# A new hand-written emission order between the last lags and the first feed-forward block, and the skip term of the last two chunks added in PSUM

## The chip, the cores and the metric

The kernel runs on one core of a Trainium2 chip. The metric is device time of one execution in microseconds; lower is better. The core's engines are TensorE (PE: matmuls into PSUM, with its weight loads listed apart as PEld), VectorE (DVE: elementwise work), ScalarE (ACT: activations, copies with a scale), GpSimd (POOL) and SyncE (SP), which here issues nearly all DMAs. Each engine works through its own queue in order, and engines wait for each other by semaphores.

## The reference, cut to what matters

Two layers are run one after the other, each a state-space convolution and a SwiGLU block, both with a layer norm in front and a residual. L = 2048 positions, D = 512 channels, F = 1376 hidden columns, N = 128 states. Both layers share their weights.

```python
def _A_ref(u, ...):                       # u: (1, L, D)
    K = einsum("dn,dnl,dn->dl", Cc, exp(dt * A * l), dt * Bc).real    # (D, L) taps
    y = causal convolution of u with K along L, by FFT of length 2L
    return y + u * Dskip

def _B_ref(x, w_gate, w_up, w_down):
    return (silu(x @ w_gate) * (x @ w_up)) @ w_down

x = x + _A_ref(_layernorm(x), ...)
x = x + _B_ref(_layernorm(x), ...)
x = x + _A_ref(_layernorm(x), ...)
x = x + _B_ref(_layernorm(x), ...)
```

The skip term `u * Dskip` is the same as `Dskip` added to tap 0 of K, and that is how the kernel does it.

## The kernel before, in words

**Tiling.** Positions go in four blocks of 512 for each layer; the eight blocks are worked in the order `SEQ`, (layer, block): (0,0), (0,1), (0,2), (1,0), (0,3), (1,1), (1,2), (1,3). The convolution is done block by block with odd-frequency transforms of length 1024 as matmuls: the spectra of the taps and of the normed inputs are multiplied on DVE and transformed back on PE. Each spectrum is cut by channel half `h` (256 channels) and by frequency residue `q`, worked in the order 0, 2, 1, 3. A feed-forward block goes in two halves of 256 positions (`TB`); for each half PE makes gate and up products in PSUM (`pgu`), two hidden tiles at a time (L934, L935, L937: three half-precision products for one of near-single precision), then the down products `py` (L950 to L952).

**Taps.** The taps come in eight chunks of 64 channels. For each chunk DVE and ACT make powers; PE multiplies them to the lags, `pk` (`lags`, L514); ACT copies them to `ks` (`spread_in`, L525). For the first six chunks `ks` goes through DRAM to its final place `kt`. For the last two, 6 and 7, `spread_pe` does it: 16 products of 256 columns with slices of the identity move partition groups into the PSUM tile `kp` (L541), and ACT copies `kp` to `kt` (L543). Then `skip` (L521) adds `Dskip` to tap 0, which lies in partition 0: on DVE for chunks 0 to 6, on POOL for chunk 7. PE transforms `kt` to spectra: `spectra` for two residues at once (L549, combined on DVE in L577), `first_parts` (L594, copied by ACT in L595) for the part that block 0 needs, `later_parts` (L603, L605, which run L549) for the parts of the later blocks. The second variable that `later_parts` yields at is the point between the halves: one call of `take` emits products of the real part, the next those of the imaginary part, the third the combination (four ACT copies L612, L613, one DVE add L614, a store by SP).

**The stretch that is reordered** begins after `pk` of chunk 7 is emitted (L1175) and ends with the last line of the hand-written order (L1256). In it stand, as generators that `take(it, n)` advances by n steps:

- `conv[h]`: the convolution of block 0 for half `h`. Each of the first four steps makes one residue's product on DVE (L816, L824, L825); every second step adds L771 and L772. The fourth makes two inputs of the inverse transform (L837, then L840, L841) and has PE transform each (`pi`, L788). The fifth makes the other two (L845, L848, L849) and adds the first result to `x` (L797); the sixth adds the second.
- `tail["sp"]`: the end of `spectra` of chunk 6 (the add L577, then two stores).
- `first_parts(c, q)`: `c` is 7. The call for chunk 7 with q = 0 or 2 covers chunk 7; that for chunk `c - 1` with q = 1 or 3 covers chunks 6 and 7. `conv[1]` needs all four, its residues in the order q = 0, 2, 1, 3.
- `odd` and `rest`: `later_parts` of chunk 6 (q = 1, 3: six steps) and of chunk 7 (all q: twelve steps).
- `split(hi, lo, load)`: steps of preparing the feed-forward weights as two half-precision parts: a load by SP, the high part on ACT (L677; the first on DVE, L675), the residue on DVE (L682). Eight column groups come first, then eleven row groups of `w_down` (L702, L705), which are emitted after the stretch.
- `scales` and `tops`: small DVE work for the weights' scales (L359, L364 to L376). `last`: the last normed input's spectrum of block 1 (PE L316, ACT L319).
- `norm`: the layer norm ahead of the first feed-forward half: DVE statistics, a power on POOL (L214), the last factor on DVE (L217); then ACT's scaling (L868), PE's transposes (L870) and ACT's copy to `nh` (L873); then DVE's residue `nlo` (L875).
- `block1`: the convolution of block 1; its first step makes one residue's product.
- `direct_size`, `sizes`: maxima for a scale.

**What sets the order.** In the stretch PE, DVE, ACT and POOL take their instructions in the order in which the code emits them (`manual_schedule`). SP and everything emitted later are placed by the framework's planner, which simulates a timeline and can put later work between instructions of the hand-written order. Of the PSUM tiles, `kp`, `pt` and `pgu` share two large buffers (`pbig`), and the pieces of `later_parts`, the inverses and `pf` share two tags of two small ones (`psml`), which alternate from call to call:

```python
small = [itertools.cycle(("sml", "py"))]
def psml(shape, name):
    return ps.tile(shape, F32, name=name, tag=next(small[0]), bufs=2)
```

Of the kernel before, what the change touches and what calls it, by code (L numbers as in the profile page):

```python
# [32 lines left out]
DC = 64  # L33
NCH = D // DC
# [43 lines left out]
def kernel(ctx, tc, x, a_re, a_im, b_re, b_im, c_re, c_im, log_dt, d_skip,  # L78
                           w_gate, w_up, w_down, c_ef, c_ei, c_ek, c_am, c_eh, c_eih, out):
    nc = tc.nc  # L80
    V, A, G, PE = nc.vector, nc.scalar, nc.gpsimd, nc.tensor
# [9 lines left out]
    def tl(shape, name, tag, dt=F32):  # L91
        return sb.tile(shape, dt, name=name, tag=tag, bufs=BUFS[tag])

    def pbig(shape, name):
        return ps.tile(shape, F32, name=name, tag="big", bufs=2)
# [45 lines left out]
    ident = sb.tile([P, P], F32, name="ident")  # L141
# [49 lines left out]

    tdk = tl([P, 2, D], "tdk", "t")
    dsk, th32 = tdk[0:1, 0], tdk[:, 1]
    nc.sync.dma_start(dsk, d_skip)
    dmax = sb.tile([1, 1], F32, name="dmax")

    def direct_size():

        da = tl([1, D], "da", "sg")
        A.activation(da, dsk, AF.Abs)  # L200
        V.tensor_reduce(dmax, da, axis=AX.X, op=OP.max)
# [45 lines left out]
    def parted(t):  # L247

        return t.rearrange("p a b d -> p b a d")
# [60 lines left out]
    def direct(b, h, q, n, space=psml):  # L310

        pf = space([P, 2, HD], "pf")
        for i in range(2):
            for c in range(4):
                e = ek[q // 2][:, q % 2, c - 1, i] if c else ef[:, q, i]
                PE.matmul(pf[:, i], lhsT=e, rhs=n[c], start=c == 0, stop=c == 3)  # L316
        yield
        u = tl([P, NQ, 2, DC], "u", "uu")
        A.activation(parted(u), whole(pf), AF.Copy)  # L319
        nc.sync.dma_start(udr[0][b, h, q], u)  # L320
# [3 lines left out]
    def second(h, q, space=psml):  # L324
        if h not in halves:
            halves[h] = n = []
            for cp in range(2):
                t = tl([P, 2, HD], "n1", "uu")
                nc.sync.dma_start(t, ndr[h, cp])
                n += [t[:, 0], t[:, 1]]  # L330
        return direct(1, h, q, halves[h], space)
# [175 lines left out]
    def lags(ts, g):  # L507
        re, im = ts[:2]
        pk = pbig([P, 16, 64], "pk")
        for i, e in enumerate((re, im)):  # L510
            for dd in range(16):
                for grp in range(4):
                    d = 16 * grp + dd
                    PE.matmul(pk[32 * grp:32 * grp + 32, dd, :], lhsT=g[:, i, :, d], rhs=e[:, 0:64, d], start=i == 0 and dd % 8 == 0, stop=i == 1 and dd % 8 == 7,  # L514
                              tile_position=(0, 32 * grp))
        return pk

    def skip(ch, kt, eng):

        k = kt[0:1, :, 0]  # L520
        eng.tensor_tensor(k, k, dsk[:, ch * DC:(ch + 1) * DC].rearrange("p (g d) -> p g d", g=4), OP.add)  # L521

    def spread_in(pk):
        ks = tl([P, 4, 16, 16], "ks", "nn")
        A.activation(ks, pk.rearrange("p d (c a) -> p a c d", a=4), AF.Copy)  # L525
        return ks

    def spread(ch, ks, kt, eng=nc.sync):

        k = kdr[ch % 2]  # L530
        with tc.high_priority(offset=BOOST):
          eng.dma_start(k.rearrange("g b a f -> (g b) a f"), ks.rearrange("p a c d -> p a (c d)"))
          for ga in range(4):
            eng.dma_start(kt[32 * ga:32 * ga + 32].rearrange("p g c d -> p g (c d)"), k[:, :, ga].rearrange("g b f -> b g f"))

    def spread_pe(ks, kt):

        kp = pbig([P, 4, 16, 16], "kp")
        for grp in range(4):
            for ga in range(4):  # L540
                PE.matmul(kp[32 * ga:32 * ga + 32, grp], lhsT=ident[:, 32 * grp:32 * grp + 32], rhs=ks[:, ga],  # L541
                          start=True, stop=True, tile_position=(0, 32 * ga))
        A.activation(kt, kp, AF.Copy)  # L543

    def products(pw, kt, k0, k1, q, order):
# [41 lines left out]
    def first_parts(c0, q):  # L587

        n = NCH - c0
        pw = pbig([P, 2, 8, 4, 16], "pw")[:, :, :n]  # L590
        for c in range(4):
            for i in range(2):
                e = ek[q // 2][:, q % 2, c - 1, i] if c else ef[:, q, i]
                PE.matmul(pw[:, i], lhsT=e, rhs=kt2[:, c0 + 2 - NCH:, :, c], start=c == 0, stop=c == 3)  # L594
        A.activation(parted(w0r[:, 1, q, c0 % NQ:]), pw.rearrange("p i k g d -> p i k (g d)"), AF.Copy)  # L595
# [23 lines left out]
    def sizes(ch, kt, junk):  # L619

        A.activation(junk, kt, AF.Abs, accum_out=wsum[:, ch:ch + 1])
# [20 lines left out]
    def take(it, n):  # L642
        for _ in range(n):
            next(it, None)
# [101 lines left out]
    def ssm(layer, b):  # L746

        if (layer, b) == SEQ[INV]:
            nc.sync.dma_start(eih, c_eih)
        for h in range(2):  # L750
            yield from ssm_half(layer, b, h)
# [227 lines left out]
    with tc.manual_schedule(engines={mybir.EngineType.Activation, mybir.EngineType.DVE, mybir.EngineType.PE, mybir.EngineType.Pool}):  # L979
# [56 lines left out]
        def at(t, f, n=1):  # L1036
            plan.append((t, len(plan), (lambda: take(f, n)) if hasattr(f, "__next__") else f))

        def later(make):

            yield from make()
# [35 lines left out]
        def use(c, t):  # L1077

            box, kt, n = {}, kt2[:, c % 2], starts[c + 1]

            def copy():
                box["ks"] = spread_in(box["pk"])
                if c < NCH - 2:
                    spread(c, box["ks"], kt)
            at(t, lambda: box.update(pk=lags(ts[c], gs[c])))
            at(t + 7.1, copy)
            if c == NCH - 2:
                at(t + 10.0, lambda: spread_pe(box["ks"], kt))
            at(t + 13.1, lambda: skip(c, kt, V))
            at(t + 25.0, lambda: sizes(c, kt, box["ks"]))  # L1090
            for q0, ats in list(enumerate(((t + 17.5, t + 25.2, n + 2.1, n + 7.5),
                                      (n + 6.9, n + 14.0, n + 17.3, n + 21.0))))[:2 if c < NCH - 2 else 1]:
                sp = later(lambda q0=q0: spectra(c, kt, q0))
                if c == NCH - 2:
                    tail["sp"] = sp
                    ats = ats[:2]
                for t0 in ats:
                    at(t0, sp)
# [26 lines left out]
        tail = {}  # L1125
        starts = [0.0, 31.0, 62.0] + [93.0 + 28.0 * k for k in range(NCH)]
        for i in range(NCH - 1):
            t = starts[i]
# [12 lines left out]
        t = starts[NCH - 1]  # L1141
# [8 lines left out]
        c, kts = NCH - 1, (kt2[:, 0], kt2[:, 1])  # L1150
# [5 lines left out]
        nhl2 = mix[:, 4 * D:].bitcast(F16).rearrange("p (s i k t) -> p s i k t", s=2, i=2, k=4)  # L1156
# [9 lines left out]
        def split(hi, lo, load=0):  # L1166
            for _ in range(load):
                loads.pop(0)()
            for _ in range(hi):
                his.pop(0)()  # L1170
            for _ in range(lo):
                los.pop(0)()
# [9 lines left out]
        conv = [ssm_half(0, 0, h) for h in range(2)]  # L1182
# [7 lines left out]
        ks = spread_in(pk)  # L1190
        odd = later_parts(c - 1, kts[0], (1, 3))
        rest = later_parts(c, kts[1])
# [2 lines left out]
        ivs = iv[0] + iv[1]  # L1195
        norm = first_norm(tl([P, 2, D], "nn1", "hf"))
        last = second(*sec[-1])
        take(conv[0], 1)
        take(tail["sp"], 2)
        spread_pe(ks, kts[1])  # L1200
        skip(c, kts[1], G)
        take(conv[0], 1)
        while tops:
            tops.pop(0)()
        scales()
        split(1, 0)
        first_parts(c, 0)
        take(conv[0], 1)
        split(1, 1)
        split(0, 0, 1)  # L1210
        first_parts(c, 2)
        split(1, 0)
        take(conv[0], 1)
        first_parts(c - 1, 1)
        split(1, 0)
        take(last, 2)
        take(conv[1], 1)
        first_parts(c - 1, 3)
        take(conv[1], 1)
        split(0, 1)  # L1220
        split(0, 0, 1)
        take(conv[0], 1)
        take(conv[1], 1)
        split(1, 1)
        split(0, 0, 1)
        take(conv[1], 1)
        split(0, 1)
        split(0, 0, 1)
        take(odd, 2)
        take(conv[1], 1)  # L1230
        direct_size()
        block1 = ssm(0, 1)
        take(norm, 1)
        take(rest, 2)
        take(odd, 1)
        take(odd, 2)
        take(norm, 1)
        take(block1, 1)
        take(rest, 1)
        split(1, 0)  # L1240
        take(odd, 1)
        take(norm, 1)
        split(0, 1)
        take(rest, 3)
        take(conv[0], 1)
        take(conv[1], 1)
        ready = nhl2[:, 0, 0], nhl2[:, 0, 1]
        split(1, 1)
        take(rest, 3)
        split(1, 1)  # L1250
        take(rest, 4)
        split(0, 0, 3)
        sizes(c, kts[1], ks)
        nn2 = tl([P, 2, D], "nn2", "nn")
        nt3 = sb.tile([P, D], F16, name="nt3")
        parts = itertools.cycle([nn2[:, 1].bitcast(F16)[:, i * D:(i + 1) * D] for i in range(2)] + [nt3])  # L1256
# [54 lines left out]
```

## Time and profile before

| what | us |
|---|---|
| median of three runs (1073.61 to 1075.19) | 1075.15 |
| the profiled execution, whole | 1072.84 |
| its span, first to last instruction | 1071.1 |
| PE busy in the span | 1016.9 |
| DVE busy | 964.0 |
| ACT busy | 546.3 |
| POOL busy | 107.5 |

The profile gives each engine's instructions with start, duration and the releaser of the idle time before them. Matmuls are pipelined, so a row's duration is longer than its share of PE's time; the distance between two starts is what counts. A single-precision matmul shows as two rows. The table of windows gives the busy time in a stretch and the clock that was granted to PE (1.00 is full).

### The profile page before, as it was taken

What the parts mean: (1) busy time and instruction counts of PE and PEld (TensorE: products, weight loads), DVE (VectorE), ACT (ScalarE), POOL (GpSimd) and SP (SyncE); (2) the same over time, 40 slices, a digit from 0 to 9 for tenths busy, and PEclk for the clock granted to TensorE, in tenths of its full rate; (3) what the DMA queues carried; (4) which work ended last, traced back from release to release, by engine and by line L of the source; (5) the groups of instructions that cost most, each with busy time, mean ns of one, the idle gap of its engine ahead of it and who ended that gap; (6) DMA issues with size and microseconds to landing.
All of it is one profiled execution on the core that took longest, in us unless ns stands there. A gap on an engine that the chain in (4) does not pass through costs nothing.

```text
span 1071.1 us, 22000 instructions
## 1 busy us (share of the span) xinstructions
PE 1016.9 (95%) x8918; PEld 801.9 (75%) x8918; DVE 964.0 (90%) x1397; ACT 546.3 (51%) x1093; POOL 107.5 (10%) x169
## 2 busy tenths in 40 slices
PE   1979999998788999999999999999999999999998
PEld 1868888887686787777869687786868677696775
DVE  7999999999999999999999999999999999972221
ACT  6989888853367264466652126534526522153210
POOL 1112322320001011011000000200100000000000
PEclk9989999998899999999999999999999999999999
DMA  6366777878755354423054454453533344312000
GB/s 216 105 187 167 176 164 186 191 194 268 250 176 166 105 149 114 148 94 80 20 124 144 142 191 132 103 148 104 149 110 94 100 137 128 119 32 58 2 26 20
DMA packets 120199, 139.73 MB, mean 130 GB/s; under 512 B 50705, under 2 KB 75793, under 8 KB 119330
## 3 DMA queue, kind: packets, MB, share of 16 engines
q1 hardware_dynamic: 108098, 112.83, 35.1%
q0 software_dynamic: 12000, 25.50, 10.1%
q8 instruction: 70, 1.15, 0.5%
q14 instruction: 31, 0.25, 0.1%
HBM read 91.36 MB, written 30.67 MB: 114 GB/s over the span
## 4 chain that ended last, share of the span: by engine, by line
PE 58%; DVE 29%; ACT 5%; issue 3%; DMA 3%; POOL 1%; SPq 0%; DVEq 0%; ACTq 0%
PE pgu L934 10%; PE pgu L935 10%; PE pgu L937 10%; PE py L952 6%; PE py L951 6%; PE py L950 6%; DVE g L489 4%; PE pi L788 3%; DVE g L504 2%; DVE spare L501 2%; PE pf L284 2%; DVE wall L416 2%; DVE t L816 2%; PE pw L549 1%; DVE yk L819 1%
## 5 line engine op out<-in xcount | busy, mean ns | idle before, releaser
L934 PE MATMUL pgu<-mix,wall 128*128 128x256 f16 x1280 | 299.7, 273 | 1.6 <-ACT mix L873 1.1
L935 PE MATMUL pgu<-mix,wall 128*128 128x256 f16 x1280 | 299.5, 273 | 0.0
L937 PE MATMUL pgu<-mix,wall 128*128 128x256 f16 x1280 | 195.8, 273 | 0.0
L935 PEld LDWEIGHTS <-wall 128*128 128x128 f16 x1280 | 125.5, 98 | 17.9 <-issue 2.4
L934 PEld LDWEIGHTS <-wall 128*128 128x128 f16 x1280 | 125.4, 98 | 15.1
L937 PEld LDWEIGHTS <-wall 128*128 128x128 f16 x1280 | 125.2, 98 | 15.0
L950 PE MATMUL py<-wall,hh 128*128 128x512 f16 (+1 forms) x352 | 133.4, 379 | 0.0
L951 PE MATMUL py<-wall,hh 128*128 128x512 f16 (+1 forms) x352 | 133.4, 379 | 0.0
L952 PE MATMUL py<-wall,hl 128*128 128x512 f16 (+1 forms) x352 | 132.4, 379 | 0.0
L819 DVE TENSOR_TENSOR yk<-yk,t 128x1024 f32<-128x1024 f32 x96 | 116.9, 1218 | 0.4
L816 DVE TENSOR_TENSOR t<-uu,w 128x1024 f32<-128x1024 f32 x96 | 116.9, 1218 | 0.3
L940 ACT ACTIVATE sg<-pgu,sc 128x512 f32<-128x512 f32 x80 | 54.6, 682 | 98.1 <-PE pgu L937 95.1
L942 ACT ACTIVATE hh<-sg 128x512 f16<-128x512 f32 x80 | 50.2, 627 | 102.0 <-DVE sg L941 102.0
L941 DVE SCALAR_TENSOR_TENSOR sg<-pgu,sc,sg 128x512 f32<-128x512 f32 x80 | 59.6, 745 | 40.4 <-ACT sg L940 40.4
L549 PE MATMUL pw<-kt,ek 128*128 128x256 f32 (+1 forms) x384 | 94.0, 383 | 0.0
L549 PEld LDWEIGHTS pw<-kt,ek 128*128 128x128 f32 x384 | 75.4, 200 | 8.6
L952 PEld LDWEIGHTS <-hl 128*128 128x128 f16 (+1 forms) x352 | 34.3, 98 | 38.5
L943 DVE TENSOR_TENSOR hl<-sg,hh 128x512 f16<-128x512 f32 x80 | 54.9, 686 | 8.9 <-ACT hh L942 8.8
L951 PEld LDWEIGHTS <-hh 128*128 128x128 f16 (+1 forms) x352 | 34.5, 98 | 37.8
L950 PEld LDWEIGHTS <-hh 128*128 128x128 f16 (+1 forms) x352 | 34.4, 98 | 37.5
L514 PE MATMUL pk<-wall,g 128*32 128x64 f32 x2048 | 58.7, 287 | 1.9 <-issue 1.8
L514 PEld LDWEIGHTS pk<-wall,g 128*32 128x32 f32 x2048 | 55.9, 134 | 5.1 <-issue 5.0
(273 smaller groups left out, 1845.2 us busy)
## 6 DMA issues: line engine op xcount, KB each, us to landing
uu<-udr SPq DMA_DIRECT2D x96, 256.0 KB, 3.0
w<-wdr SPq DMA_DIRECT2D x96, 256.0 KB, 2.8
g<-g POOLq DMA_DIRECT2D x12, 512.0 KB, 7.2
udr<-fu POOLq DMA_DIRECT2D x22, 256.0 KB, 3.2
udr<-u SPq DMA_DIRECT2D x16, 256.0 KB, 3.3
kdr<-ks SPq DMA_DIRECT2D x6, 512.0 KB, 3.4
kt<-kdr SPq DMA_DIRECT2D x24, 128.0 KB, 3.1
out_dram<-xg SPq DMA_DIRECT2D x12, 256.0 KB, 2.3
```

Of the source, the lines that this page charges most:

```text
L514: PE.matmul(pk[32 * grp:32 * grp + 32, dd, :], lhsT=g[:, i, :, d], rhs=e[:, 0:64, d], start=i == 0 and dd % 8 == 0, stop=i == 1 and dd % 8 ...
L549: PE.matmul(pw[:, i], lhsT=e, rhs=kt[:, :, c + 4 * k0:4 * k1:4, :].rearrange("p g k d -> p k g d"), start=c == 0, stop=c == 3)
L816: V.tensor_tensor(t, uu.unsqueeze(2).to_broadcast([P, NQ, 2, 2, DC]), w.unsqueeze(3).to_broadcast([P, NQ, 2, 2, DC]), OP.mult)
L819: V.tensor_tensor(yk, yk, t, OP.add)
L934: PE.matmul(o, lhsT=wgu(wi, k, 0)[:, fs], rhs=nh[:, k], start=k == 0, stop=False)
L935: PE.matmul(o, lhsT=wgu(wi, k, 1)[:, fs], rhs=nh[:, k], start=False, stop=False)
L937: PE.matmul(o, lhsT=wgu(wi, k, 0)[:, fs], rhs=nlo[:, k], start=False, stop=k == 3)
L941: V.scalar_tensor_tensor(sg, pgu[:, 1], sc6[:, 4:5], sg, OP.mult, OP.mult)
L943: V.tensor_tensor(hl[:, f0:f0 + 2], sg, hh[:, f0:f0 + 2], OP.subtract)
L950: PE.matmul(py[r], lhsT=hh[:n, f, rc], rhs=wd(f, 0)[:n], start=f == 0, stop=False)
L951: PE.matmul(py[r], lhsT=hh[:n, f, rc], rhs=wd(f, 1)[:n], start=False, stop=False)
L952: PE.matmul(py[r], lhsT=hl[:n, f, rc], rhs=wd(f, 0)[:n], start=False, stop=f == FT - 1)
```

## The change

The skip term of chunks 6 and 7 is no longer added by DVE and POOL: `spread_pe` adds it in PSUM, by one more product for each of the four groups. For that the part of `tdk` that holds `Dskip` in its first row is cleared on POOL before the load. The order of the stretch is written anew, one step to a line; the number of steps of each kind is the same, except that what `take` asks for beyond an iterator's end does nothing.

```diff
     dsk, th32 = tdk[0:1, 0], tdk[:, 1]
+    G.memset(tdk[:, 0], 0.0)
     nc.sync.dma_start(dsk, d_skip)
...
-    def spread_pe(ks, kt):
+    def spread_pe(ch, ks, kt):
         kp = pbig([P, 4, 16, 16], "kp")
         for grp in range(4):
             for ga in range(4):
                 PE.matmul(kp[32 * ga:32 * ga + 32, grp], lhsT=ident[:, 32 * grp:32 * grp + 32], rhs=ks[:, ga],
-                          start=True, stop=True, tile_position=(0, 32 * ga))
+                          start=True, stop=ga > 0, tile_position=(0, 32 * ga))
+                if ga == 0:
+                    PE.matmul(kp[:32, grp, 0], lhsT=ident[:, :32], rhs=tdk[:, 0, ch * DC + 16 * grp:ch * DC + 16 * (grp + 1)],
+                              start=False, stop=True, tile_position=(0, 0))
         A.activation(kt, kp, AF.Copy)
...
-                at(t + 10.0, lambda: spread_pe(box["ks"], kt))
-            at(t + 13.1, lambda: skip(c, kt, V))
+                at(t + 10.0, lambda: spread_pe(c, box["ks"], kt))
+            if c < NCH - 2:
+                at(t + 13.1, lambda: skip(c, kt, V))
```

The order of steps, before and after, with `take(x, 1)` written as the name of `x`:

```text
before: conv0, sp, sp, spread_pe, skip (POOL), conv0, tops, scales, split hi, first_parts(c,0), conv0,
  split hi lo, load, first_parts(c,2), split hi, conv0, first_parts(c-1,1), split hi, last, last, conv1,
  first_parts(c-1,3), conv1, split lo, load, conv0, conv1, split hi lo, load, conv1, split lo, load,
  odd, odd, conv1, direct_size, norm, rest, rest, odd, odd, odd, norm, block1, rest, split hi, odd, norm,
  split lo, rest x3, conv0, conv1, split hi lo, rest x3, split hi lo, rest x4, load x3, sizes
after: conv0, sp, tops, scales, spread_pe, first_parts(c,0), conv0, split hi, split hi, conv0, sp, split lo,
  first_parts(c-1,1), first_parts(c,2), conv0, split hi, conv1, last, last, split lo, load, conv1, conv0,
  conv1, split hi, split hi, load, first_parts(c-1,3), split lo, split lo, load, load, odd, odd, conv1,
  conv1, odd, direct_size, norm, rest, rest, odd, conv1, rest, odd, block1, rest, split hi, norm, norm, odd,
  rest, split lo, rest, split hi, rest, split lo, conv0, rest, split hi, rest, split lo, load, load, rest,
  load, rest, sizes, rest
```

More of the change, by code (lines that the diff above doesn't have):

```diff
@@ L1197 @@
         last = second(*sec[-1])
+        ready, block1 = (nhl2[:, 0, 0], nhl2[:, 0, 1]), ssm(0, 1)
         take(conv[0], 1)
[L1199 to L1202, printed above, removed]
+        take(tail["sp"], 1)
         while tops:
@@ L1205 @@
         scales()
-        split(1, 0)
+        spread_pe(c, ks, kts[1])
         first_parts(c, 0)
         take(conv[0], 1)
-        split(1, 1)
-        split(0, 0, 1)
-        first_parts(c, 2)
+        split(1, 0)
         split(1, 0)
         take(conv[0], 1)
+        take(tail["sp"], 1)
+        split(0, 1)
         first_parts(c - 1, 1)
+        first_parts(c, 2)
+        take(conv[0], 1)
         split(1, 0)
-        take(last, 2)
         take(conv[1], 1)
-        first_parts(c - 1, 3)
-        take(conv[1], 1)
+        take(last, 1)
+        take(last, 1)
         split(0, 1)
         split(0, 0, 1)
+        take(conv[1], 1)
         take(conv[0], 1)
         take(conv[1], 1)
-        split(1, 1)
+        split(1, 0)
+        split(1, 0)
         split(0, 0, 1)
-        take(conv[1], 1)
+        first_parts(c - 1, 3)
+        split(0, 1)
         split(0, 1)
         split(0, 0, 1)
-        take(odd, 2)
+        split(0, 0, 1)
+        take(odd, 1)
+        take(odd, 1)
         take(conv[1], 1)
+        take(conv[1], 1)
+        take(odd, 1)
         direct_size()
-        block1 = ssm(0, 1)
         take(norm, 1)
-        take(rest, 2)
+        take(rest, 1)
+        take(rest, 1)
         take(odd, 1)
-        take(odd, 2)
-        take(norm, 1)
+        take(conv[1], 1)
+        take(rest, 1)
+        take(odd, 1)
         take(block1, 1)
@@ L1240 @@
         split(1, 0)
+        take(norm, 1)
+        take(norm, 1)
         take(odd, 1)
-        take(norm, 1)
+        take(rest, 1)
         split(0, 1)
-        take(rest, 3)
+        take(rest, 1)
+        split(1, 0)
+        take(rest, 1)
+        split(0, 1)
         take(conv[0], 1)
[L1246 to L1252, printed above, removed]
+        take(rest, 1)
+        split(1, 0)
+        take(rest, 1)
+        split(0, 1)
+        split(0, 0, 1)
+        split(0, 0, 1)
+        take(rest, 1)
+        split(0, 0, 1)
+        take(rest, 1)
         sizes(c, kts[1], ks)
+        take(rest, 1)
         nn2 = tl([P, 2, D], "nn2", "nn")
```

## The prediction

> **What bounds the kernel now.** First the page's span, then the waits of TensorE (PE) from 329 us to the end, then a table of windows. Its columns are the stretch, then for each engine busy us and instructions, then the granted PE clock.
>
> ```profile
> span 1071.1 us, 22000 instructions
> ```
> ```profile
> PE pgu L934 <- DVE sg L941: 0.3, 1, 0.3
> PE pgu L934 <- DVE sg L912: 0.3, 1, 0.3
> ```
> ```profile
> 236.00:258.40 22.40, 18.44 (x325) 14.66 (x323) 21.88 (x35) 6.34 (x11) 4.29 (x6) 0.92 0.77 203
> 258.40:276.20 17.80, 17.64 (x96) 15.95 (x96) 16.93 (x27) 7.29 (x10) 0.04 (x1) 0.81 0.87 296
> 276.20:288.80 12.60, 6.59 (x32) 5.39 (x32) 11.60 (x23) 2.05 (x6) 1.34 (x1) 0.96 0.75 234
> 288.80:299.10 10.30, 9.18 (x40) 8.99 (x41) 10.20 (x14) 4.00 (x7) 0.00 (x0) 0.72 0.81 274
> 299.10:320.90 21.80, 19.88 (x144) 18.37 (x143) 20.88 (x27) 16.36 (x44) 0.00 (x0) 0.92 0.60 182
> 320.90:329.00 8.10, 3.73 (x15) 2.54 (x14) 7.91 (x16) 6.47 (x13) 3.33 (x1) 0.79 0.88 275
> 329.00:1071.00 742.00, 737.04 (x5782) 561.19 (x5780) 648.69 (x962) 305.32 (x577) 46.02 (x68) 1.00 0.35 103
> ```
>
> From 329 us on PE waits 0.6 us in 742, at clock 1.00. So the end is 329 plus the PE work that is left there, and an earlier end needs PE to have done more by then. The six windows above it, which hold all that is reordered, show what PE wastes there. Idle time is length less busy time: 4.0, 0.2, 6.0, 1.1, 1.9 and 4.4 us, together 17.6. Reduced clock costs at most length times (1 - clock): 1.8, 3.4, 0.5, 2.9, 1.7 and 1.7, together 12. Some 28 us is thus the pool that a new order can draw on. VectorE (DVE) is busy for 21.88 of 22.40, 16.93 of 17.80, 11.60 of 12.60, 10.20 of 10.30 us: it paces the stretch, and little can be won on DVE itself. What can be won is that PE's pieces stand where their inputs are ready.
>
> **The change part by part.** I follow three dates: when PE gets the first tap spectra of chunk 7, when the normed input `nh`/`nlo` of the first feed-forward block is there, and when PE has filled both PSUM buffers with `pgu`.
>
> *The skip terms.* Timeline rows of PE and POOL, with the idle time before them and its releaser:
>
> ```profile
> 237.38 0.67 PE L549 MATMUL pw<-kt,ef 128*128 128x256 f32 x2 [1.06 <-DVE kt L521]
> ...
> 244.89 7.25 PE L514 MATMUL pk<-wall,g 128*32 128x64 f32 x256
> 253.35 3.35 PE L541 MATMUL kp<-ks,ident 128*32 128x256 f32 x32 [1.20 <-ACT ks L525]
> 258.49 0.66 PE L594 MATMUL pw<-kt,ef 128*128 128x64 f32 x4 [1.79 <-POOL kt L521]
> 258.99 1.50 PE L594 MATMUL pw<-kt,ek 128*128 128x64 f32 x12
> ...
> 260.98 2.77 PE L594 MATMUL pw<-kt,ek 128*128 128x64 f32 x12
> ```
> ```profile
> 257.86 0.58 POOL L521 TENSOR_TENSOR kt<-kt,tdk 1x64 f32<-1x64 f32 x1 [18.11 <-ACT kt L543]
> ```
>
> Chunk 6: PE no longer waits 1.06 us for the add behind DVE's queue. DVE loses one short instruction, which I leave out of the sum. What is late next is `pk` (L514). It also follows a small `nrm` product that waits for ScalarE, so I move it up 0.6, not 1.06. Chunk 7: from the start of POOL's add (257.86) to L594 at 258.49 are 0.63 us, which go; PE then follows ScalarE's copy of `kt` itself. Added on PE: 4 products of 16 columns in each of the two calls. The 32 rows of `kp` come from 16 products, so they are 8 rows. The trace has none like them: L514 gives 7.25/256 = 0.03 us a row, L541 3.35/32 = 0.105, hence 0.23 to 0.84 us a call. I take 0.4 for chunk 7: the output tile is L541's, but 16 columns move instead of 256. First spectra of chunk 7: 258.49 - 0.6 - 0.63 + 0.4, about 257.7.
>
> The rule of the Trainium skill (TensorE: Matmul & The Clock Gate, section "Back-to-back issue gap") is an issue floor of about 25 ns for a small matmul; by it the estimate for 8 rows is 0.2 us, against the 0.4 taken, and L514's 28 ns a row agrees with it.
>
> The new memset is one of POOL's, at the start:
>
> ```profile
> 1.33 0.20 POOL L149 MEMSET ones<- 128x128 f32 x1
> ```
> ```profile
> 10.87 0.30 SPq L194 DMA_DIRECT2D tdk<-in_A_Dskip_dram  x1
> ```
>
> A quarter of the columns took 0.20 us, so 0.8 at most. The load of the skip vector, which has to follow it, is issued at 10.87, nine us after the row above. Nothing; without that cover 0.8 us for a load that only the finished taps need.
>
> *Block 0 on DVE, up to the norm.*
>
> ```profile
> 264.10 1.23 DVE L816 TENSOR_TENSOR yk<-mix,w0r 128x1024 f32<-128x1024 f32 x1 [0.38 <-ACT w0r L595]
> ...
> 267.49 1.64 DVE L682 SCALAR_TENSOR_TENSOR wall<-wall,sc 128x1376 f16<-128x1376 f32 x1
> ...
> 274.85 1.23 DVE L816 TENSOR_TENSOR yk<-mix,w0r 128x1024 f32<-128x1024 f32 x1 [0.22 <-ACT w0r L595]
> ...
> 279.84 0.43 DVE L840 TENSOR_TENSOR bb<-bb 128x256 f32<-128x256 f32 x1 [0.79 <-PE pi L788]
> ...
> 288.12 0.15 DVE L217 SCALAR_TENSOR_TENSOR rs<-mv,rs 128x2 f32<-128x2 f32 x1
> 288.25 0.56 DVE L614 TENSOR_TENSOR wos<-pw,wos 128x384 f32<-128x384 f32 x1
> 288.72 1.22 DVE L816 TENSOR_TENSOR yk<-u,w0r 128x1024 f32<-128x1024 f32 x1
> ...
> 302.98 1.22 DVE L875 TENSOR_TENSOR mix<-pt,mix 128x1024 f16<-128x1024 f32 x1
> ```
>
> DVE's list from 244 us to L217 (the norm's last factor) is the same (less that skip) but for one thing: the first `odd` combination (L614, 0.47 from 288.25 to 288.72) moves ahead of the norm. Its waits were 0.38, 0.22 and 0.79. The last stays: in step 4 of `conv[1]` the second product takes the tile that the first inverse still reads. The first grows, I think. `first_parts(c, 2)` is now third on PE instead of second, behind `first_parts(c - 1, 1)`, and step 2 of `conv[1]` waits for it. 12 of 16 rows took 1.50 us at full clock and 2.77 at a reduced one, so a whole group takes 1.9 or 3.7. Three from 257.7 end at 263.4 or 268.8. DVE gets to that step at 265.2 (263.7 of before, and a weight residue of 1.6 from 267.49 now ahead of it). The wait is 0 to 3.8; I take 1.1, that is, the clock falling midway as it did in the second window. The residues moved forward need ScalarE halves that stand ahead of them, and their DMAs were issued long before. Sum: 0.47 - 0.38 - 0.22 + 1.1 = 1.0, so L217 comes at 289.1. **DVE wins nothing before the norm.**
>
> *PE from there.*
>
> ```profile
> 279.10 2.35 PE L788 MATMUL pi<-bb,mix 128*128 128x256 f32 x8 [2.97 <-DVE bb L837]
> 281.29 0.49 PE L549 MATMUL pw<-kt,ef 128*128 128x192 f32 x2
> ...
> 283.89 1.89 PE L788 MATMUL pi<-bb,mix 128*128 128x256 f32 x8
> 288.86 1.01 PE L549 MATMUL pw<-kt,ef 128*128 128x192 f32 x2 [3.09 <-DVE wos L614]
> ...
> 297.01 1.04 PE L870 MATMUL pt<-ident,nn 128*128 128x128 f32 x8
> ...
> 302.06 1.01 PE L549 MATMUL pw<-kt,ef 128*128 128x192 f32 x2 [1.87 <-DVE wos L614]
> ```
> ```profile
> 298.08 1.02 ACT L873 ACTIVATE mix<-pt 128x1024 f16<-128x1024 f32 x1 [5.10 <-PE pt L870]
> ```
>
> Here is the gain. Before, PE stood 2.97 us ahead of the inverse of 279.10 and then 3.09 us for a PSUM buffer that the `odd` combination still held; after that the clock was 0.72 for a window, and the transposes of the norm (L870) stood behind four products in it. In the new order the two first `odd` products (2.60 us from 281.29 to 283.89) go ahead of the inverse, into the first gap, and their combination, now ahead of the norm, frees the buffer before `rest` asks. PE's list from 258.49 to 276.13 (where the gap of 2.97 began) holds the same pieces, so 257.7 + 17.6 + 2.6 = 277.9. DVE's input for the inverse (279.1 before) comes at 281.1: 0.5 later by the waits above, 1.5 by a residue that now stands ahead. The inverses end at 285.0, as DVE allows. Then PE runs two `rest`, two `odd` and a third `rest` half, 1.30 each: 291.5. On ScalarE the norm follows the four `rest` copies and one weight cast of 1.4 us, so the transposes end near 292.5 and `nh` is there at 293.5. Before: 298.05 and 299.10. PE has done one more half by then: ahead by 5.55 + 1.30 = 6.9 us.
>
> On DVE, `nlo` (L875) stood after block 1's first products and after what the planner put between, until 302.98. Now a result (0.6), one combination (0.5) and step 1 of block 1 stand between L217 and it, the last with three passes of 1.22 and two of 0.43 (288.72 and 279.84 show these shapes): `nlo` at 296.1. PE's remaining five `rest` halves (6.5 us) and the first `pgu` fill the time between. So the idle 1.1 at 299 (fourth window), the wait of 1.87 and the reduced clock behind them (1.7 in the fifth window, I count 1.5) go: 4.5 us.
>
> Against that: the new order leaves a gap from 277.9 to 281.1 before the inverse. Behind 3.09 us the clock cost 2.9, behind 2.97 hardly anything (8 rows in 2.35 instead of 1.89): 0 to 2.9, I take the middle, 1.4.
>
> The Trainium skill, same page, Part 1 "The HAM clock gate", has the clock halved only after an idle window of about 3.4 us. By that rule this 1.4 is not due and the sum would be 11.4 instead of 10.0, thus 1063.8 us. The row of 302.06 speaks against it: after waits of 1.1 and 1.87 its first two rows took 1.01 us, as against 0.49 at 281.29.
>
> *The first drains.*
>
> ```profile
> 313.56 0.63 ACT L227 ACTIVATE junk<-n 128x512 bf16<-128x512 f32 x1 [2.18 <-DMA n<-in_A_u_dram]
> ...
> 322.58 1.28 ACT L940 ACT_TABLE_LOAD   x1
> 323.88 0.69 ACT L940 ACTIVATE sg<-pgu,sc 128x512 f32<-128x512 f32 x1
> ```
> ```profile
> 326.03 0.73 DVE L941 SCALAR_TENSOR_TENSOR sg<-pgu,sc,sg 128x512 f32<-128x512 f32 x1
> ```
>
> Both `pgu` buffers were full at 320.9, and PE stood 4.4 us, then ran at reduced clock: 6.1 in the last window. With the lead PE is there near 310.9. Whether ACT's Silu is there as well isn't to be read from the listing, because the feed-forward is placed by the planner. I let this wait stand as it was; ends: 0, and all of the lead.
>
> **Sum:** 6.9 + 4.5 - 1.4 = 10.0 us off 1071.1 of span. The profiled execution took 1072.84 (1.74 outside the span), 0.2% under the median of 1075.15; I take the gain from the median: **1065**. The later stages can take it. The last block is the tightest:
>
> ```profile
> 959.68 0.81 ACT L886 ACTIVATE nn<-xf,rs 128x512 f32<-128x512 f32 x1 [1.14 <-DVE rs L232]
> ```
> ```profile
> 981.11 1.41 DVE L957 SCALAR_TENSOR_TENSOR xg<-py,sc,xg 128x512 f32<-128x512 f32 x2 [6.60 <-PE py L952]
> ```
>
> Its norm starts at 959.7, and PE comes to it when the block before is drained, at 981: some 16 us to spare after the norm and its transposes.
>
> **The rivals.**
>
> *A, the drains keep their date.* ACT's row statistics (L227, from 313.56, after 2.18 us for the load of `n`) were queued ahead of the Silu. If they are again, they end near 318 and Silu comes with its table load at 319 to 320, L941 at 322 instead of 326: PE waits, the gain is 4, **1071**. For it: the load hangs on DVE's residues, not on PE. Against: the Silu has the higher priority as soon as its `pgu` is planned done.
>
> *B, the wait for drains goes as well.* ACT's listed work after `nh` (three combinations' copies, two casts, a size) is about 8 us, so Silu could start at 301 to 303. Then 6.1 more: **1059**, and by the 16 us of the last block hardly less.
>
> *C, the change doesn't bring the norm forward.* The planner puts block 1's products into DVE ahead of L875, as it did from 294 to 302. `nlo` then comes at 302, PE stands after its `rest` halves, and no more than the skip's 0.7 remains: **1074.5**.
>
> *D, slower: PE falls to half clock in the new order.* PE's work from 257.7 to 292.5 is about 28 us at full clock (17.6 - 3.4, 2.6, two pairs of inverses at 1.9, five halves at 1.3, transposes at 1.0); I charge 4.8 of loss (3.4 and 1.4). Each further us at half clock that DVE then waits for moves all behind it. With 15 of the 28 us at half clock the gain is gone; with 20 it is 5 slower, **1080**. For it: the clock fell after every gap but one, and three groups in a row now stand ahead of what DVE waits for. Against: fewer gaps.
>
> **How the numbers follow.** Forecast (1061 to 1069) 0.43, A 0.18, B 0.12, C 0.13, D 0.14. A measurement tells some 0.2% (2.1 us) from no change: forecast, A and B are faster, 0.73; C the same, 0.13; D slower, 0.14. The range reaches from B's 1058 to 1077, just past C; left out are most of D and the end of B.
>
> **What would show it.** First L594 of chunk 7 with no POOL row ahead, at 257 to 258; L816 of `conv[1]` waiting about 1 us for `w0r`; no wait of `pw` for L614 between 284 and 300; L873 ended by 294 and L875 by 297; a clock of 0.9 or more from 288 to 299; the first Silu before 320. I am wrong if L875 stays after 301 (C), if the first `pgu` drain stays at 326 (A), or if PE waits again after 329 for more than 1 us.

## The result and the profile after

The changed kernel takes 1065.74 us (median of 6 runs, 1063.59 to 1066.60), the kernel before, run beside it, 1074.62 (6 runs). The ratio is 0.992, with a 95% interval of 0.9909 to 0.9931: 8.6 us faster, between 7.4 and 9.8. 1065 was forecast. The profiled execution took 1066.60 with this span:

```profile
span 1064.8 us, 22047 instructions
```

So the profiled spans differ by 6.3 us (1071.1 before), less than the 8.6 of the medians: the profiled execution of after is the slowest of its six, that of before lies 1.8 us under its median. First the same table of windows as before, with the time from 329 to 990 us cut into three (behind 990 PE is busy without a gap in both); columns are the stretch, busy us and instructions of PE, its weight loads, DVE, ACT and POOL, then the granted PE clock.

```profile
236.00:258.40 22.40, 20.03 (x358) 17.48 (x357) 21.92 (x35) 7.04 (x15) 4.16 (x5) 1.00 0.79 216
258.40:276.20 17.80, 15.45 (x89) 13.84 (x89) 17.56 (x26) 7.30 (x9) 0.00 (x0) 0.90 0.85 315
276.20:288.80 12.60, 9.86 (x37) 7.86 (x37) 10.52 (x23) 1.60 (x5) 1.32 (x1) 0.73 0.58 193
288.80:299.10 10.30, 10.30 (x73) 10.04 (x72) 9.73 (x12) 10.14 (x20) 0.00 (x0) 1.00 0.79 273
299.10:320.90 21.80, 21.80 (x183) 18.59 (x181) 21.80 (x34) 19.10 (x43) 0.70 (x1) 1.00 0.65 216
320.90:329.00 8.10, 8.10 (x67) 5.96 (x65) 7.07 (x12) 8.07 (x18) 1.21 (x2) 1.00 0.67 180
329.00:700.00 371.00, 367.27 (x2884) 281.20 (x2883) 366.38 (x557) 172.25 (x334) 31.01 (x44) 1.00 0.41 120
700.00:960.00 260.00, 260.00 (x2057) 199.21 (x2056) 255.37 (x364) 92.93 (x173) 14.96 (x19) 1.00 0.38 112
960.00:990.00 30.00, 26.60 (x192) 19.66 (x191) 10.04 (x18) 16.89 (x34) 1.39 (x2) 0.89 0.29 58
```

The first and the last of those three, of before:

```profile
329.00:700.00 371.00, 371.00 (x2919) 283.88 (x2918) 367.33 (x560) 182.44 (x351) 34.61 (x46) 1.00 0.41 119
...
960.00:990.00 30.00, 30.00 (x219) 20.79 (x217) 8.21 (x14) 12.35 (x24) 0.90 (x2) 1.00 0.24 56
```

Read them as an account of PE. Ahead of 329 us the idle time fell from 17.6 to 7.5 us (2.4, 2.4 and 2.7 in the first three windows, none from 288.8 on), and the bound on lost clock (length times one less the clock) from 12 to 5.2 (1.8 and 3.4). That is 10.1 + 6.8 = 16.9 us won. Behind 329 us, where before had 0.6 us of waits (in the prediction), after has 3.7 + 3.4 = 7.1, and 30 x 0.11 = 3.3 of lost clock: some 10 us given back. The account leaves about 7, against 6.3 of span. **The change wins some 16 us and gives 10 back**, and the dates say the same. The first result of a feed-forward block, of after, on DVE (L957 in the numbering of before):

```profile
350.64 0.74 DVE L961 SCALAR_TENSOR_TENSOR xg<-py,sc,xg 128x512 f32<-128x512 f32 x1
...
968.64 1.40 DVE L961 SCALAR_TENSOR_TENSOR xg<-py,sc,xg 128x512 f32<-128x512 f32 x2
```
and of before (the row of 981.11 stands in the prediction):
```profile
366.92 0.74 DVE L957 SCALAR_TENSOR_TENSOR xg<-py,sc,xg 128x512 f32<-128x512 f32 x1
```

PE is 16.3 us ahead at the first result, 12.5 at the last block, 6.3 at the end. What PE waits for behind 329 us, of after; columns are the waiting tile and line, the releaser, the sum, the count and the longest:

```profile
PE pgu L907 <- DMA mix<-nn: 2.4, 2, 1.3
PE pgu L938 <- DVE sg L916: 1.6, 2, 0.9
PE pgu L909 <- DMA mix<-nn: 1.0, 1, 1.0
PE pgu L909 <- DMA mix<-nt: 1.0, 1, 1.0
PE pi L792 <- DVE yl L237: 0.6, 1, 0.6
PE pgu L938 <- DVE sg L945: 0.5, 1, 0.5
```

Two kinds: drains of `pgu` and one split of an inverse's input on DVE (2.7 us, all ahead of 700 us), and transposed norms (L907, L909; 4.4 us). 1.0 of the latter falls at 496 us, 3.4 at the last block's first half. Of that norm ACT's first statistics row, of after, then of before:

```profile
961.35 0.63 ACT L228 ACTIVATE nn<-xf 128x512 f32<-128x512 f32 x1
```
```profile
954.10 0.63 ACT L227 ACTIVATE nn<-xf 128x512 f32<-128x512 f32 x1
```

Before, it began 27 us ahead of PE's arrival (981.1). Now PE arrives 12.5 us earlier and the norm begins 7.3 us *later*, and PE has to wait.

### The profile page after: what moved, and what is told of

The parts are those of the page before. It is cut to its first block, busy times and chain, and to the rows that moved or that the text cites. A ratio compares the mean times of both kernels' runs of the same rounds, so it can differ in the third digit from the quotient of the medians.

```text
span 1064.8 us, 22047 instructions
## 1 busy us (share of the span) xinstructions
PE 1015.1 (95%) x8934; PEld 800.4 (75%) x8934; DVE 962.4 (90%) x1396; ACT 545.1 (51%) x1093; POOL 107.5 (10%) x169
## 4 chain that ended last, share of the span: by engine, by line
PE 46%; DVE 20%; issue 4%; ACT 3%; DMA 1%; POOL 0%; DVEq 0%; ACTq 0%; POOLq 0%
PE pgu L938 9%; PE pgu L939 9%; PE pgu L941 9%; PE py L954 5%; PE py L955 5%; PE py L956 5%; DVE yk L820 3%; DVE t L820 2%; PE pi L792 2%; DVE yk L823 2%; PE pf L285 1%; DVE sg L945 1%; DVE hl L947 1%; DVE yl L237 1%; DMA hl<-sg 1%
## 5 line engine op out<-in xcount | busy, mean ns | idle before, releaser
L941 PE MATMUL pgu<-mix,wall 128*128 128x256 f16 x1280 | 196.4, 273 | 0.0
L941 PEld LDWEIGHTS <-wall 128*128 128x128 f16 x1280 | 125.5, 98 | 14.7
```

The lines of the kernel that those rows point to most:

```text
L941: PE.matmul(o, lhsT=wgu(wi, k, 0)[:, fs], rhs=nlo[:, k], start=False, stop=k == 3)
```

## The experiments

Two theories for the ten microseconds given back. **T1**: the new order wins its 16 us, but DVE, busy for 366.38 of 371.00 and 255.37 of 260.00 us, has no slack, and its date for the last block's norm sets the end. **T2**: PE's own work bounds the kernel to the end. All ratios are to the kernel before, run beside each kernel.

### The two parts alone

Order_only has the new order with the skip terms added as before; skip_only has the PSUM skip in the order of before.

Order_only, against after:

```diff
-        spread_pe(c, ks, kts[1])
+        spread_pe(ks, kts[1])
+        skip(c, kts[1], G)
```

Skip_only, against before:

```diff
-        spread_pe(ks, kts[1])
-        skip(c, kts[1], G)
+        spread_pe(c, ks, kts[1])
```

> The new order of steps, with the skip term as before: DVE adds it for chunk 6, POOL for chunk 7 right after spread_pe. Theory 1 (PE leads by some 16 us when the first feed-forward block ends, and the last block, which waits for DVE's last convolution, takes back what is over about 9): the skip's 0.7 us is taken from a lead that is too long anyway, so the time is that of the changed kernel within 1 us, 1065 to 1067. Theory 2 (PE's lead goes to the end, and the time lost behind 329 us is lost to waits that the planner's new placing brought by chance): 0.7 to 1.2 us above the changed kernel, 1066.5 to 1067. The first py result (L957 of before, 366.9 us there, 350.6 in the changed kernel) at 351 to 352 in both.

> The order of before, with the skip term of chunks 6 and 7 added in PSUM. PE waits 1.06 us less ahead of the spectra of chunk 6 and about 2 less for chunk 7 (the changed kernel has its first L598 at 255.8, before had it at 258.5). But conv steps behind it are DVE's, which has no time to win there. Both theories: 0 to 1.1 us under before, 1073.5 to 1074.6; the order then carries nearly all of the gain.

Order_only took 1068.09 us, 0.9938 (0.9923 to 0.9952); skip_only 1070.86, 0.9962 (0.9948 to 0.9976). So the order alone is worth 6.7 us and the skip alone 4.1 (2.6 to 5.6), more than the 1.1 at most that was expected: a miss. Order_only's median lies above the ranges of both theories, and its distance from after, 1.9 us with an interval of about 2, doesn't tell them apart. Together the two parts give 8.6, not 10.8; with intervals of 1.2 to 1.6 us on each of the three, that difference isn't clear of the noise. What came of the skip, in a window of skip_only and its first spectra:

```profile
236.00:258.40 22.40, 20.03 (x360) 17.71 (x359) 21.88 (x35) 6.52 (x13) 3.74 (x5) 1.00 0.83 227
```
```profile
255.36 0.66 PE L598 MATMUL pw<-kt,ef 128*128 128x64 f32 x4 [1.16 <-ACT kt L547]
```

The clock stayed at 1.00 there and in the next window, where before had 0.92 and 0.81, and the first spectra came 3.1 us earlier (258.49 before). The clock gave the next question.

### Is it the clock?

Before_warm puts products that nobody reads into PE's two waits around the spreading of chunk 7 in the kernel before.

```diff
+    def warm(n):
+        dm = [psml([P, P], "dm") for _ in range(2)]
+        for i in range(n):
+            PE.matmul(dm[0], lhsT=ident, rhs=ident, start=True, stop=True)
...
+        warm(7)
         spread_pe(ks, kts[1])
+        warm(12)
         skip(c, kts[1], G)
```

> Before, with 19 products of the identity with itself (128x128 fp32) that nobody reads: 7 in TensorE's wait ahead of the seventh chunk's spreading (1.2 us), 12 in its wait behind it (1.8 us). Theory C1, for the 3.4 us that the PSUM skip alone won where at most 1.1 were expected: the rest came from the granted clock, which fell to 0.92 and 0.81 in 236 to 276 us before and stayed at 1.00 there with the PSUM skip, because the wait behind the spreading is shorter. Then filling the waits wins 1 to 3 us here: 1071.5 to 1073.5. Theory C2: the gain came from VectorE's and GpSimd's relief, and the clock was that run's chance: 0 to 1 us slower than before, for the dummy products that outlast the waits.

1074.68 us, 0.9994 to 1.0015 of before (1.0005). The edit did what it was meant to do to the clock, in the first window (1.00) and in the second:

```profile
258.40:276.20 17.80, 14.32 (x98) 13.14 (x97) 17.41 (x28) 7.99 (x11) 0.00 (x0) 1.00 0.90 315
```

and nothing came of it. Nor did it where the clock of the first window was 1.00 by itself, in two kernels below that are before with an edit elsewhere (before_dve and before_pt; neither is faster than before). **C1 falls** as the whole cause: PE then waits for DVE, with 3.5 us idle in that second window where before had 0.2, and the faster clock only lengthened the waits; it was also lower behind (0.73 in the third window, 0.84 in the fifth, before 0.96 and 0.92).

One thing before_warm didn't repeat: the dummy products held PE until 258.43, so the first spectra came when they do in before, and not 3.1 us earlier. But in other traces the first result doesn't follow that date. In before_dve (below) the first spectra came at 257.06 and the first result at 367.61, no earlier than before (366.92); in order_only they came at 258.20 and the first result at 350.77, within 0.2 us of after. What skip_only's trace does show is that PE no longer stands for the first drains: the window ahead of 329 us, and the first Silu, which came 6.4 us earlier (323.88 before).

```profile
320.90:329.00 8.10, 8.10 (x65) 6.11 (x63) 8.10 (x15) 8.10 (x22) 0.00 (x0) 1.00 0.69 247
```
```profile
317.47 0.69 ACT L944 ACTIVATE sg<-pgu,sc 128x512 f32<-128x512 f32 x1
```

Its first result came at 365.05, 1.9 us ahead of before, while the norm's factor didn't move (288.11, before 288.12). Why the Silu came earlier no run tells, so the cause of the skip's 4.1 us stays open.

### More work for PE, more work for DVE

Four halves of `rest` computed twice (5.2 us of PE) in after and in before; four of DVE's products for block (1,0) computed twice (4.9 us) in both. Each second copy overwrites the first. (T3, where an expectation names it, has DVE's load count in before as well.)

In after_pe and before_pe (and the same for the imaginary half):

```diff
-            products(pw, kt, 1, NB, q, [(0, c) for c in range(4)])
+            for _ in range(2 if ch == NCH - 1 and q % 2 else 1):
+                products(pw, kt, 1, NB, q, [(0, c) for c in range(4)])
```

In after_dve and before_dve:

```diff
-                V.tensor_tensor(t, uu.unsqueeze(2).to_broadcast([P, NQ, 2, 2, DC]),
-                                w.unsqueeze(3).to_broadcast([P, NQ, 2, 2, DC]), OP.mult)
+                for _ in range(2 if (layer, b, h, k) == (1, 0, 0, 0) else 1):
+                    V.tensor_tensor(t, uu.unsqueeze(2).to_broadcast([P, NQ, 2, 2, DC]),
+                                    w.unsqueeze(3).to_broadcast([P, NQ, 2, 2, DC]), OP.mult)
```

> The changed kernel with four of the eight later_parts halves of chunk 7 (q = 1 and 3) computed twice, 4 x 1.30 = 5.2 us more PE work behind the norm's transposes; the result is the same. Theory 1: PE's lead falls from 16 to 11 us, which still is more than the last block can use, so the time grows by 0 to 1.5 us (1066 to 1067). Theory 2: PE is the bound all the way, plus 5.2 us (1071).

> The kernel before with the same four later_parts halves of chunk 7 computed twice (5.2 us more PE work in the stretch). Before, PE waits 0.6 us behind 329, and the last block's norm was there some 15 us before PE came to it. Both theories: plus 4 to 5.5 us (1078.5 to 1080), a little less where the new work fills a wait of PE.

> The changed kernel with four DVE products of block (1,0) computed twice, 4 x 1.2 = 4.9 us more DVE work at about 500 us; the result is the same. Theory 1: DVE sets the start of the last block, plus 3.5 to 5 us (1069.5 to 1071). Theory 2: DVE has time to spare, within 1 us of the changed kernel.

> The kernel before with the same four DVE products of block (1,0) computed twice, 4.9 us of DVE. Theory 1 (DVE sets the last block only once PE has its lead): within 1 us of before, where the changed kernel paid 2.3. Theory 3 (any more DVE work costs about half its time in either kernel, because DVE is busy for 99% of 329 to 945): plus 2 to 3.

| kernel | us | ratio (95%) | against its base |
|---|---|---|---|
| after_pe | 1069.63 | 0.9944 (0.9930 to 0.9958) | +2.6 of 5.2 |
| before_pe | 1076.26 | 1.0013 (1.0004 to 1.0022) | +1.4 of 5.2 |
| after_dve | 1068.71 | 0.9941 (0.9928 to 0.9953) | +2.3 of 4.9 |
| before_dve | 1073.27 | 0.9994 (0.9986 to 1.0003) | -0.6 of 4.9 |

(The last column is the difference of ratios times 1074.6; with an interval of about 2 us in after, 1 in before.) The DVE pair speaks for T1: the same work costs nothing before and about half of itself after, though T1 had asked for 3.5 to 5 us. In both it delays the norm; the rows of after_dve, then of before_dve:

```profile
966.16 0.63 ACT L228 ACTIVATE nn<-xf 128x512 f32<-128x512 f32 x1 [0.61 <-DVE xf L237]
```
```profile
960.48 0.63 ACT L227 ACTIVATE nn<-xf 128x512 f32<-128x512 f32 x1 [0.19 <-DVE xf L236]
```

4.8 and 6.4 us later. Before has PE at the last block only at 981.83 and pays nothing. After pays, in the waits of PE in after_dve:

```profile
PE pgu L908 <- DMA mix<-nn: 4.8, 2, 4.5
```

In the PE pair, after_pe's 2.6 us lie between T1, which wanted at most 1.5, and T2, which wanted 5.2; the interval of 2 us leaves out T2's figure, but not T1's. In after_pe the wait for the norm is gone, since PE came to the last block only at 976.12 (after: 968.64); it waits for drains instead:

```profile
PE pgu L940 <- DVE sg L947: 3.5, 3, 2.3
```

Before_pe lost 1.4 and not 4 or more, a miss of both theories. Its trace no longer has the wait of 4.4 us for the first drains, which the added work can have filled. That isn't the whole account: its first result came 5.2 us later than before's (372.12), and PE was only 2.5 us late at the last block (983.61).

### After once more

> The changed kernel once more, on the chip and among the runs of the next three: 1065 to 1066.5, a ratio to before of 0.991 to 0.993. No theory differs here.

1066.25 us, 0.992 (0.9906 to 0.9934). The first result came at 349.8, the norm began at 960.63, and PE again waited for its transposes: the pattern isn't that of one execution.

### Relieving DVE

After_pool takes one in five of the drains' residues from DVE to POOL.

```diff
-                    V.tensor_tensor(hl[:, f0:f0 + 2], sg, hh[:, f0:f0 + 2], OP.subtract)
+                    (G if f0 == 0 else V).tensor_tensor(hl[:, f0:f0 + 2], sg, hh[:, f0:f0 + 2], OP.subtract)
```

> The changed kernel with the first of the five hl residues of each feed-forward half (L947, f0 = 0) on POOL instead of DVE: 16 x 0.6 = 9.7 us less for DVE, 14 of them ahead of the last block's norm (8.4 us). Theory 1: that norm comes some 5 to 8 us earlier and PE no longer waits for it; 2 to 5 us faster than the changed kernel (1061 to 1064). Theory 2 (PE is the bound all the way): within 1 us. If POOL's own time for one is over 2 us or DVE slows beside it, the gain is less.

1067.71 us, 0.9925 (0.9911 to 0.9938): no gain, a miss. The groups of that line, on POOL and on DVE; columns are the count, the busy time, the mean ns of one, then the idle time ahead:

```profile
L947 POOL TENSOR_TENSOR hl<-sg,hh 128x512 f16<-128x512 f32 x16 | 33.3, 2080 | 194.5 <-ACT hh L946 193.4 <-issue 1.1
L947 DVE TENSOR_TENSOR hl<-sg,hh 128x512 f16<-128x512 f32 x64 | 43.6, 681 | 6.3 <-ACT hh L946 6.2
```

POOL needs 2.08 us in the mean (1.16 to 3.88) for what DVE does in 0.68, and PE's waits for drains grew (of after_pool):

```profile
PE pgu L938 <- DVE sg L916: 4.4, 2, 3.1
```

The norm began 1.0 us earlier (960.34), not 5 to 8. The wait for it is gone here as well, because PE came to the last block at 979.20, 10.6 us later than in after: waits for drains and for splits of inputs on DVE had taken its lead before.

### The last block's norm itself

After_pt and before_pt make the transposes of the last block's first half on PE, as the first block does, and not by DMA.

```diff
+            if (layer, b) == SEQ[-1] and s == 0:
+                pt = pbig([P, rows, 4, P], "pt")
...
+                        PE.transpose(pt[:, r, k], nn2[:, 0, k * P:(k + 1) * P], ident)
...
+                A.activation(nhv, ptv, AF.Copy)
+                V.tensor_tensor(nlo.rearrange("p k (r t) -> p k r t", r=rows), ptv, nhv, OP.subtract)
+                return nh, nlo
```

> After, but the last block's first half is normalised as the first block's is: its sixteen 128x128 transposes go to TensorE through PSUM instead of through four DMA transposes. In the run of after, TensorE came to the last block at 968.6 us, the norm's statistics began at 961.35, its DMA transposes ran from 967.36 to 973.6, and TensorE waited 1.11 + 0.96 + 1.33 = 3.4 us for the drains and transposes behind them. T1 (the end is set by VectorE's date for the last block's norm, and the DMA transposes behind it): most of the 3.4 us of waits goes, less about 1 us for the transposes themselves: 3 to 4 us under after, 1062 to 1063 us. T2 (TensorE bound all the way): no gain, within 1 us of after, or 1 us over it for the transposes.

> Before with the same edit of the last block's norm as in after_pt. In the run of before TensorE came to the last block at 981 us, 15 us after the DMA transposes had ended (966.4). T1: nothing to win there, within 1 us of before, or 1 us slower for the transposes on TensorE. If it gains 3 us or more as after_pt does, then the gain of after_pt isn't that of a wait that only the new order has, and T1 falls.

After_pt: 1065.20 us, 0.9917 (0.9901 to 0.9934), no gain that can be told from none, where T1 wanted 3 to 4 us: a miss; before_pt: 1.0011 (0.9998 to 1.0023), as expected. The waits of PE at the end of after_pt say why:

```profile
PE pgu L918 <- ACT mix L897: 1.1, 1, 1.1
PE pt L894 <- ACT nn L892: 1.0, 1, 1.0
PE pgu L920 <- DVE mix L898: 0.9, 1, 0.9
```

3.0 us for the same date: on PE the transposes stood behind the block before, in PE's own order, and the second row's had to wait for the one buffer of normalised values. The wait was moved, not removed.

After_bn makes the norm itself earlier: statistics by DVE's BN_STATS, a second buffer for the normalised row, and an own buffer for the last two inverses' inputs.

```diff
+                if (layer, b, h) == (*SEQ[-1], 1) and r >= 2:
+                    yl = z2[:, r % 2].rearrange("p (l i) d -> p l i d", l=2)
...
+            last = (layer, b) == SEQ[-1] and s == 0
+            if last:
+                rs, nb = stats(xt, rows, 256.0, "stats2")
...
+            if last:
+                nf[1] = tl([P, NQ, 2, DC], "uu", "uu").rearrange("p a b c -> p (a b c)")
```

> After, with the last block's first half normalised earlier, at the same work for TensorE: its mean and variance by VectorE's BN_STATS instead of by four passes of ScalarE (4.67 us from the first pass at 961.35 to the factor's end in the run of after), a second buffer for the second row's normalised values, and the last convolution's third and fourth inverse in a buffer of their own, so that VectorE splits them while it waits (3.29 us) for TensorE's first. The norm's factor should then come some 1.5 to 2 us earlier and the second row's part 1 us more. In the run of after TensorE waits 1.11 + 0.96 + 1.33 = 3.4 us there, and the stretch 960 to 990 us has a clock of 0.89 (26.60 us busy: 2.9 us). T1 (what was given back at the end is the wait for this norm): 2 to 3.4 us of waits go, and as much as 2.9 us of clock: 1.5 to 5 us under after, 1061 to 1064.5, with TensorE's waits for the norm under 1.5 us. T2 (the waits there cost nothing, the end is TensorE's work alone): within 1 us of after. After_pt moved the same wait to the transposes on TensorE, so it couldn't tell.

1064.40 us, 0.9908 (0.9890 to 0.9925): the lowest median of the study, 1.3 us under after by the ratios, but the intervals overlap. The factor came 2.7 us earlier (963.18, after: 965.66), and the stretch 960 to 990 kept its clock:

```profile
960.00:990.00 30.00, 26.87 (x216) 20.25 (x214) 10.68 (x22) 12.77 (x24) 1.39 (x2) 1.00 0.27 58
```
```profile
PE pgu L916 <- DMA mix<-nn: 1.5, 2, 0.9
PE pgu L918 <- DMA mix<-nt: 1.0, 1, 1.0
PE pgu L918 <- DMA mix<-nn: 0.7, 1, 0.7
```

PE still waits 3.2 us where T1 wanted less than 1.5. PE also came earlier, and the four transposes now hold it up one by one, each 1.2 us on the DMA queue, with two stores between them. So 3.3 us of lost clock are gone from the trace and the waits are nearly as they were; that the gain is real can't be claimed from these runs.

**What is settled.** That after wins some 16 us up to its first result, and that 10 go again, is read off the traces of after and after_again. That DVE's load has become a cost, which it wasn't before, is shown by after_dve and before_dve, for work added at one place. That the last norm's date alone sets the end (T1 as first put) is not: in after_pe and after_pool PE came later than the norm and had waited for drains on the way, in after_pt the wait was moved, and none was faster. T2 fails by the 7.1 us of PE's idle time behind 329 and by after_pe. What remains, as a reading, is that PE and DVE both have next to no slack, and whichever is relieved waits for the other.

## Why the prediction was right, and where not

The time and the sign were right, and the range (1058 to 1077) held it. Of the sum's terms, several were off, and two large errors cancelled by luck.

*What bounds.* Right: PE's waste in six windows was the pool, and the gain was drawn from it.

*The skip.* Rows of PE, of after:

```profile
252.47 0.65 PE L542 MATMUL kp<-ks,ident 128*32 128x256 f32 x8 [1.20 <-ACT ks L526]
252.93 0.21 PE L545 MATMUL kp<-tdk,ident 128*32 128x16 f32 x2
252.99 0.64 PE L542 MATMUL kp<-ks,ident 128*32 128x256 f32 x8
...
255.79 0.66 PE L598 MATMUL pw<-kt,ef 128*128 128x64 f32 x4 [1.16 <-ACT kt L547]
```

First spectra at 255.79, not 257.7; no POOL row ahead. The added product takes 252.93 to 252.99, 0.06 us for its two rows: 0.24 for the call, at the low end of the 0.23 to 0.84, of which 0.4 was taken. The estimate from the Trainium skill (TensorE: Matmul & The Clock Gate, "Back-to-back issue gap") was 0.2, and the trace agrees. Some 1.4 of the 1.9 us are the clock: the spreading, the added products in it, took 2.15 us at full clock (252.47 to 254.62), where 3.35 + 0.24 would be due at the reduced clock of before, which I had kept. The clear of `tdk` took 0.52 us on POOL and was hidden.

*DVE up to the norm.* The wait of 1.1 for `first_parts(c, 2)` didn't come: with the three groups at full clock from 255.8 to 261.2 the low end (0) was the right one. DVE waited elsewhere, 1.38 and 0.43 us for the inverse. The norm's factor came at 288.56 (289.1 forecast, 288.12 before): **DVE wins nothing before the norm** was right.

*PE from there.* The wait ahead of the inverse and what followed it, of after:

```profile
268.95 3.52 PE L792 MATMUL pi<-bb,mix 128*128 128x256 f32 x8 [2.35 <-DVE bb L849]
...
279.59 6.73 PE L792 MATMUL pi<-bb,mix 128*128 128x256 f32 x16 [2.74 <-DVE bb L841]
286.16 0.49 PE L553 MATMUL pw<-kt,ef 128*128 128x192 f32 x2
...
292.66 1.04 PE L874 MATMUL pt<-ident,nn 128*128 128x128 f32 x8
```

The gap of 277.9 to 281.1 was there as 276.85 to 279.59. It cost the upper end of what was bounded: 16 rows in 6.6 us, where two times 1.89 is due at full clock, 2.8 more, and not 1.4. By the rule of the Trainium skill (TensorE: Matmul & The Clock Gate, Part 1 "The HAM clock gate"), a clock that falls only after an idle window of some 3.4 us, nothing was due; the measured rows decide, after waits of 2.35 and 2.74 us. The `odd` products filled the gap as forecast, the wait for L614 went, and the transposes began at 292.66, where I had them end near 292.5. That is 4.35 us earlier than before (297.01), and PE had one more half of 1.30 done: 5.65, where 6.9 - 1.4 = 5.5 was forecast. From there the stretch has no idle time and clock 1.00, so the 4.5 us of the next term came too. `nh` followed at 295.3 and not 293.5, since three weight casts (L706, 1.94 us) were put ahead of it, and `nlo` at 298.2 and not 296.1, on DVE; PE had enough `rest` halves to cover both:

```profile
296.99 1.22 DVE L879 TENSOR_TENSOR mix<-pt,mix 128x1024 f16<-128x1024 f32 x1
```

*The first drains: the first step that failed.* "I let this wait stand as it was" took the 4.4 us wait and its 1.7 of clock as unmoved. Of after:

```profile
302.83 1.28 ACT L944 ACT_TABLE_LOAD   x1
304.13 0.69 ACT L944 ACTIVATE sg<-pgu,sc 128x512 f32<-128x512 f32 x1
```

The Silu came 19.8 us earlier (323.88 before), ahead of the row statistics, and PE never stood: rival B's mechanism, given 0.12. With it the front won the forecast 10.0 and 6.3 more; by the windows, 10.8 up to 320.9 us and 6.1 in the last one.

*"The later stages can take it": the second.* The 16 us to spare at the last block were measured from the norm of before, as if its date were fixed. It moved 7.3 us later. DVE was as busy as before. With PE earlier, drains come earlier and stand ahead of more of DVE's convolution work, so that the last convolution ends later: that is how I read it. DVE's rows up to its first split of inputs of that convolution's inverses (L236 at 949.21 before, L237 at 955.27 after) bear it out: 193 drain steps (L912, L914, L941, L943 and L957 in the numbering of before) stand ahead of it instead of 186, beside 1159 other instructions instead of 1158, and DVE was idle some 3 us longer. After that split it waited 3.29 us for PE's inverse, 0.65 before. The DVE pair shows that the norm's date follows DVE's load. It doesn't follow PE's lead alone, though: in skip_only the norm began 6.5 us later as well (960.56), with a lead of 1.9 us at the first result. No run changed the planner's order alone. Of the 16.3 us, 10 went, 3.7 of them in waits up to 700 us and the rest at the last norm with its lowered clock. Had I seen the first error alone, I would have said 1059, with rival B, and been wrong. So the mechanism of the front is right, its size was too small by 6 and the give-back missing; that the number is right to 1 us is luck.

*The rivals.* A (drains keep their date) and C (norm not forward) didn't happen; D's reduced clock came for the inverses of 268.95 and 279.59; its cost, 1.6 + 2.8 = 4.4 us, is near the 4.8 charged in the sum, though in other places, and far from the 15 from which it would eat the gain. "PE waits again after 329 for more than 1 us" was named as a sign of being wrong, and it is the one that showed.

## What to carry to other kernels

When PE's time is to be won in one stage, look up the busy share of the engine next to it in all that follows: at 98%, as here, its dates aren't fixed but moved when PE's did, and a lead of 16 us shrank to 6. Slack measured as "this was ready so long ahead" held only for the old order. In these runs a wait that was taken away at the end of such a chain was replaced by the next link; look at the sum of PE's waits and lost clock over the whole rest, not at the one named.

## What the runs showed of the hardware

The granted clock isn't a property of the program. The second window of after_again

```profile
258.40:276.20 17.80, 14.69 (x93) 13.22 (x91) 17.56 (x26) 8.11 (x13) 0.00 (x0) 1.00 0.87 318
```

is at 1.00, where the same program had 0.90 in the run of after. The instructions up to 258 us are the same in after, after_dve and after_pe. The first window of after_pe

```profile
236.00:258.40 22.40, 20.03 (x345) 16.62 (x344) 21.92 (x35) 6.35 (x12) 3.86 (x5) 0.92 0.79 219
```

is at 0.92 (after_pe), where after has 1.00, with the same 20.03 us busy; after_dve has 0.97. The Trainium skill (TensorE: Matmul & The Clock Gate, "The HAM clock gate") calls the activity window free-running, so that the phase varies from run to run; these rows agree. A lowered clock came with far shorter waits than the idle window of some 3.4 us that the Trainium skill gives there, though: three of 1.11, 0.96 and 1.33 us at the last block, with a clock of 0.89 over 960 to 990, while in after_bn four of 0.6 to 1.0 us left it at 1.00.
